# An attention and squared-ReLU kernel: k of tile 0 on ScalarE's queue, distances ahead of identities, six warm-up matmuls

## The chip, the core and the metric

The kernel runs on one core of a Trainium2 chip. The metric is the device time of one execution in microseconds (us). The core's engines run side by side, each with its own list of instructions: TensorE (PE, with its weight loads as PEld), VectorE (DVE), ScalarE (ACT), GpSimd (POOL) and SyncE (SP). They wait for one another, and for transfers, through semaphores. SP, ScalarE and GpSimd can issue transfers (DMAs), which 16 DMA engines then carry out. Line numbers such as L393 are lines of the kernel before; in the changed kernel the same code stands one line earlier from the identities on, or further where it says so.

## What is computed

Windowed causal attention with a linear distance bias, then two matrix products with a squared ReLU between them. Batch 4, 8 heads, 768 positions, 64 elements a head; w_in is 512 x 2048, w_out 2048 x 512. A query sees the 96 latest keys, and the first 8 keys of its sequence:

```python
rel = pos[:, None] - pos[None, :]
is_global = pos[None, :] < n_global          # 8
is_local = (rel >= 0) & (rel < n_local)      # 96
dist = np.where(is_global & ~is_local, n_local, np.abs(rel))
scores = q @ k.T / sqrt(64) - slopes[h] * dist
scores = np.where(is_global | is_local, scores, -1e9)
a = softmax(scores)
x = (a @ v)  # heads side by side: 3072 x 512
out = np.maximum(x @ w_in, 0.0) ** 2 @ w_out # 3072 x 512
```

## The kernel before

The 3072 rows are 24 tiles of 128. For each tile the kernel loads q, k and v, transposes q and k on TensorE (later ones by DMA) into a buffer qkT, makes scores with the tile's own keys and with those of the tile before, exponentiates them on ScalarE, multiplies with v, and normalizes into x on VectorE. Two tiles make a block of 256 rows; for each of the 12 blocks x goes through w_in and w_out, nearly always as seven products of halves in place of eight, which costs VectorE sums and differences and saves TensorE work. Nothing is scheduled at run time: a long table, ORDER, lists every operation of this main part and so fixes the order on every engine. The change leaves that table as it is.

Ahead of the main part stand the preparations, and these the change touches. In the order of the code:

- Tile 0 is loaded as fp32, q and k in one loop (L340), into the buffer plain; both transfers were issued by SP. A small transfer named touch follows (L347). All other q, k and v go through GpSimd's queue, which casts them to bf16; those of the first six tiles are issued at L327.
- VectorE clears a buffer (L382) and sets columns of ones (L385), GpSimd makes a table of position differences, pbi (L388). ScalarE runs a dummy exponential (L390), ahead of which its table is loaded.
- TensorE multiplies the cleared buffer with itself NWARM times, 128 x 512 (L393). The results are not used.
- VectorE makes from pbi two biased copies, pbt (L396) and pbw (L399), the fp32 and the bf16 identity (ident32, printed as ident_96, L402, and ident, L403), and pb, the masked distance, as the smaller of pbt and pbw (L404). pb0 is its own-keys half for a first tile (L406, L408), and a memset gives the global keys their distance in pb (L407). Eight scaled identities sid (L411) add the bias by a matmul (L600) in the first three tiles.
- ScalarE makes E, the exponentials of the distances times the slopes (L418, eight instructions), which later tiles multiply in on VectorE.

The main part begins on TensorE with the transposes of tile 0 (L531, operations tr.0.0 for q and tr.1.0 for k, fp32 with ident32), the bias of tile 0 (L600), transposes of q of tiles 2 and 1, and the scores of tile 0 (L621). ScalarE copies the transposed k (L450), VectorE the transposed q (L452). The transposes of k of tile 1 follow, then the bias of tile 1, the transposes of k of tile 2 and the scores of tile 1. The buffers pbi, pbt, pbw and sid lie inside the buffers named early, and so are printed under that name.

Of the kernel before, what the change touches and what calls it, by code (L numbers as in the profile page):

```python
# [16 lines left out]
Alu = mybir.AluOpType  # L17
# [148 lines left out]
def kernel(  # L166
# [11 lines left out]
    nc = tc.nc  # L178
# [9 lines left out]
    n_global = int(n_global)  # L188
    n_local = int(n_local)
# [26 lines left out]
    def const(shape, dt, name):  # L216
        return consts.tile(shape, dt, name=name, tag=name)
# [26 lines left out]
    pb = const([P, 2, P], BF16, "pb")  # L244
# [5 lines left out]
    pbt = early[:, 0, 2 * P :].rearrange("p (a c) -> p a c", a=2)  # L250
    pbw = early[:, 1, : 2 * P].rearrange("p (a c) -> p a c", a=2)
# [26 lines left out]
    NBUF, NPART = 16, 4  # L278
    SQA = {3, 6}
    NSUM = 2  # L280
    NWARM = 8
    NLATE = 2
    CUT = 3 * d_model // 4
    TWO = (0, 2)
# [35 lines left out]
    def src_rows(x, j):  # L320
        b, t = divmod(j, TPB)
        return x[b, :, t * P : (t + 1) * P, :]
# [14 lines left out]
    for j in range(NPLAIN):  # L337
        for n, src in ((0, q), (1, k)):
            t_ = plain_all[:, n]
            nc.sync.dma_start(  # L340
                out=t_.rearrange("p (h d) -> p h d", h=H),
                in_=src_rows(src, j).rearrange("h p d -> p h d"),
            )
            plain[n, j] = t_
            land["qk"[n], j] = 4.5 + 1.1 * n
# [45 lines left out]

    for i in range(NWARM):
        nc.tensor.matmul(out=banks[7], lhsT=zero[:, :P], rhs=zero, start=True, stop=True)  # L393
# [3 lines left out]
        out=pbt, in0=pbi, scalar=MASK_VAL, in1=pbi, op0=Alu.mult, op1=Alu.min  # L397
    )
    nc.vector.tensor_scalar(  # L399
        pbw, pbi, float(n_local - 1), -MASK_VAL, op0=Alu.add, op1=Alu.mult  # L400
    )
    nc.vector.tensor_scalar(ident32, pbi[:, 0, :], 0.0, None, op0=Alu.is_equal)  # L402
    nc.vector.tensor_scalar(ident, pbi[:, 0, :], 0.0, None, op0=Alu.is_equal)  # L403
    nc.vector.tensor_tensor(out=pb, in0=pbt, in1=pbw, op=Alu.min)  # L404

    nc.vector.tensor_copy(pb0, pb[:, 0, :])  # L406
    nc.vector.memset(pb[:n_global, 1, :], float(-n_local))  # L407
    nc.vector.tensor_scalar_max(pb0[:n_global, :], pb0[:n_global, :], float(-n_local))  # L408
    for h in range(H):

        nc.vector.scalar_tensor_tensor(  # L411
            out=sid[h], in0=ident32, scalar=float(slopes[h] / scale), in1=ident32,
# [68 lines left out]
    for j in range(NT):  # L481
# [152 lines left out]
        for gs in SETS.get(j, [tuple(range(groups))]):  # L634
            n = 8 * len(gs)
# [746 lines left out]
    for blk in range(NBLK):  # L1382
# [12 lines left out]
        for s, sub, half in order2:  # L1395
# [28 lines left out]
            n = NSTEP * blk + s  # L1424
# [74 lines left out]
```

## Time and profile before

| | us |
|---|---|
| median of 3 runs (lowest, highest) | 197.62 (197.32, 198.61) |
| the profiled execution, its own time | 197.03 |
| its span, first to last instruction | 195.3 |
| TensorE busy in the span | 188.3 |
| VectorE busy | 177.0 |
| ScalarE busy | 158.6 |
| GpSimd busy | 75.1 |

The profile shows one execution. The span is shorter than the device time by what lies around it, 1.73 us. A row of the list in order of time gives the start, the length, the engine, the line, the operation, its output and input and how many such instructions it gathers; in square brackets stands how long the engine was idle ahead of it, and what ended that. The ends of matmuls are modelled, so weight loads (PEld) show TensorE's pace better than matmuls do. A row of SPq is the issue of a transfer, not the transfer.

### The profile page before, as it was taken

The page shows a single profiled execution, that of the slowest core. Times are in us where ns is not written, and L with a number is a line of the kernel's source. Part 1 is how long each engine was busy: PE and PEld are TensorE (multiplying, and loading weights), DVE is VectorE, ACT ScalarE, POOL GpSimd, SP SyncE. Part 2 cuts the span into 40 slices and gives each one's busy share as a digit, 9 for nine tenths or more (in the row PEclk, how much of TensorE's full clock was granted, in tenths as well). Part 3 has the DMA queues.
Part 4 walks back from the last instruction along what each step waited for, and adds up shares of the span by engine and source line. Part 5 has one row for each costly group of instructions (what it writes and reads, how often), then busy time and mean ns, then how long its engine had stood idle before and what let it go on. Part 6 is the DMA issues. An engine that isn't in the chain of part 4 may idle for free.

```text
span 195.3 us, 6863 instructions
## 1 busy us (share of the span) xinstructions
PE 188.3 (96%) x2808; PEld 171.1 (88%) x2808; DVE 177.0 (91%) x395; ACT 158.6 (81%) x331; POOL 75.1 (38%) x93
## 2 busy tenths in 40 slices
PE   7986999999999999999999999999999999999993
PEld 3865999999889989989989999998888999999882
DVE  8478999999999999999999999978999999998960
ACT  6798899999989897999997968675987979666511
POOL 8999965747575039056230009290000000000000
PEclk9999999999999999999999999999999999999999
DMA  8999999999999999999999349999855402100055
GB/s 130 149 155 174 177 201 202 204 159 158 179 159 126 147 161 191 136 240 135 142 240 84 77 91 104 198 171 206 166 104 118 134 5 57 54 3 0 0 192 187
DMA packets 111713, 26.92 MB, mean 138 GB/s; under 512 B 103234, under 2 KB 108866, under 8 KB 111682
## 3 DMA queue, kind: packets, MB, share of 16 engines
q0 software_dynamic: 80256, 13.37, 91.9%
q1 hardware_dynamic: 31426, 13.11, 32.2%
q8 instruction: 22, 0.36, 0.7%
q14 instruction: 9, 0.07, 0.1%
HBM read 27.26 MB, written 6.29 MB: 172 GB/s over the span
## 4 chain that ended last, share of the span: by engine, by line
PE 82%; DVE 10%; ACT 3%; DMA 2%; issue 1%; ACTq 0%
PE bank L1019 32%; PE bank L1279 32%; PE bank L1140 5%; PE bank L621 5%; PE bank L774 4%; DVE x L809 2%; DVE hsum L1234 2%; DMA xT<-x 2%; PE bank L393 2%; DVE buf L712 2%; PE bank L531 2%; ACT early L687 1%; ACT buf L687 1%; DVE xs L988 1%; DVE early L712 1%
## 5 line engine op out<-in xcount | busy, mean ns | idle before, releaser
L1279 PEld LDWEIGHTS <-hsum 128*128 128x128 bf16 x384 | 35.9, 98 | 3.9
L450 ACT COPY buf<-bank 128x512 f32<-128x512 f32 (+1 forms) x56 | 30.8, 564 | 10.0 <-PE bank L1019 5.8
L1279 PE MATMUL bank<-wsum,hsum 128*128 128x256 bf16 x288 | 37.7, 273 | 0.0
L687 ACT ACTIVATE buf<-bank 128x512 bf16<-128x512 f32 x54 | 30.1, 604 | 2.3 <-PE bank L621 2.3
L1019 PEld LDWEIGHTS <-qk_first 128*128 128x128 bf16 x504 | 30.7, 98 | 1.4 <-DVE xs L988 0.3
L1086 ACT ACTIVATE hs<-buf 128x512 bf16<-128x512 f32 x46 | 28.7, 636 | 3.5 <-DVE buf L1064 3.2
L1019 PEld LDWEIGHTS <-win 128*128 128x128 bf16 x504 | 30.8, 98 | 0.8
L1064 DVE CUSTOM_DVE_ANT_0 buf<-bank,buf 128x512 f32<-128x512 f32 x42 | 28.3, 684 | 1.8 <-ACT early L687 0.7
L1279 PEld LDWEIGHTS <-hs 128*128 128x128 bf16 x288 | 26.7, 98 | 2.7
L331 POOL DMA_DIRECT2D qk<-in_q_dram x18 | 16.0, 889 | 30.1 <-DMA qkT<-qk 25.7
L1279 PE MATMUL bank<-wout,hs 128*128 128x256 bf16 x192 | 26.0, 273 | 0.0
L1019 PE MATMUL bank<-xT,win 128*128 128x128 bf16 x336 | 24.3, 219 | 0.0
L1019 PE MATMUL bank<-xs,qk_first 128*128 128x128 bf16 x336 | 24.1, 219 | 0.2 <-DVE xs L988 0.2
L331 POOL DMA_DIRECT2D v<-in_v_dram x18 | 16.1, 898 | 20.5 <-DVE hsum L1234 14.3
L687 ACT ACTIVATE early<-bank 128x512 bf16<-128x512 f32 x34 | 19.2, 612 | 2.8 <-PE bank L621 2.7
L809 DVE TENSOR_TENSOR x<-bank,rs 128x512 bf16<-128x512 f32 x24 | 16.6, 692 | 0.9
L331 POOL DMA_DIRECT2D qk<-in_k_dram x18 | 16.2, 898 | 2.3 <-DMA wout<-in_moe_w_out_dram 2.3
L1234 DVE TENSOR_TENSOR hsum<-hs 128x1024 bf16<-128x1024 bf16 (+1 forms) x26 | 16.7, 643 | 0.0
L450 ACT COPY part<-bank 128x256 f32<-128x256 f32 x31 | 11.6, 376 | 5.8 <-PE bank L1279 5.6
L1354 DVE TENSOR_TENSOR buf<-bank,part 128x256 f32<-128x256 f32 x29 | 12.1, 419 | 3.6 <-PE bank L1279 3.3
L621 PEld LDWEIGHTS <-qkT 64*128 64x128 bf16 x352 | 10.0, 94 | 3.9 <-issue 2.6
L1279 PE MATMUL bank<-wout,hsum 128*128 128x256 bf16 x96 | 13.3, 273 | 0.0
(93 smaller groups left out, 379.8 us busy)
## 6 DMA issues: line engine op xcount, KB each, us to landing
out_dram<-buf SPq DMA_DIRECT2D x17, 256.0 KB, 2.5
v<-in_v_dram POOLq DMA_DIRECT2D x24, 128.0 KB, 5.6
qk<-in_q_dram POOLq DMA_DIRECT2D x18, 128.0 KB, 4.8
qk<-in_k_dram POOLq DMA_DIRECT2D x18, 128.0 KB, 5.4
wout<-in_moe_w_out_dram POOLq DMA_DIRECT2D x8, 256.0 KB, 10.2
win<-in_moe_w_in_dram POOLq DMA_DIRECT2D x6, 256.0 KB, 6.7
out_dram<-early SPq DMA_DIRECT2D x5, 256.0 KB, 2.8
qk_first<-in_q_dram POOLq DMA_DIRECT2D x5, 128.0 KB, 4.4
```

The costliest lines, as they stand in the source:

```text
L331: nc.gpsimd.dma_start(out=dst, in_=src)
L450: nc.scalar.copy(dst, src)
L621: nc.tensor.matmul(out=tiles["sc", j, odd, g][:, at, :], lhsT=left[j - 1][half, pair, :] if kt else qkT[j % NKT][half, 1, pair, :], rhs=qk ...
L687: nc.scalar.activation(out=tiles[tag, j, g][:, odd], in_=tiles.pop(("sc", j, odd, g)).rearrange("p a c -> p (a c)"), func=Act.Exp, scale=s ...
L809: nc.vector.tensor_tensor(out=x.rearrange("p (b a) c -> p b a c", b=2), in0=po[:, :, :, :D], in1=rs.to_broadcast([P, 2, 4, D]), op=Alu.mult,)
L1019: nc.tensor.matmul(out=tiles["h", blk, g, bank][:, n], lhsT=left_[:, s, k], rhs=right_[:, k], start=opens and n == 0 and k == 0, stop=k == ...
L1064: nc.vector._custom_dve(TENSOR_ADD_SAT, out=hr, in0=src, in1=tiles.pop(("u", blk, g, i)), s0=float("inf"), s1=0.0,)
L1086: nc.scalar.activation(hs, hr, Act.Square)
L1140: nc.tensor.matmul(out=hT[:, c, cols], lhsT=w_in_sb[s][:, kt, c * P : (c + 1) * P], rhs=tiles["xT", blk][:, kt, cols], start=(kt == 0), st ...
L1234: nc.vector.tensor_tensor(out=t[:, i, h], in0=t[:, a, h] if isinstance(a, int) else half_a(blk, *a)[:, h], in1=t[:, b, h] if isinstance(b, ...
L1279: nc.tensor.matmul(out=tiles["acc", blk, bank][:, cols], lhsT=left_[:, s], rhs=right_[:, cols], start=first and s == 0, stop=s == NSTEP - ...
L1354: nc.vector.tensor_tensor(out=o_sb[:, cols], in0=tiles["acc", blk, bank][:, part], in1=tiles["part", blk, other][:, part], op=Alu.add,)
```

## The change

Three edits. The loop at L340 issues q of tile 0 on SP, as before, and k on ScalarE. NWARM goes from 8 to 6. On VectorE pb and its memset go ahead of the two identities.

```diff
-    NWARM = 8
+    NWARM = 6
...
     for j in range(NPLAIN):
         for n, src in ((0, q), (1, k)):
             t_ = plain_all[:, n]
-            nc.sync.dma_start(
+            (nc.sync, nc.scalar)[n].dma_start(
                 out=t_.rearrange("p (h d) -> p h d", h=H),
                 in_=src_rows(src, j).rearrange("h p d -> p h d"),
             )
...
+    nc.vector.tensor_tensor(out=pb, in0=pbt, in1=pbw, op=Alu.min)
+    nc.vector.memset(pb[:n_global, 1, :], float(-n_local))
     nc.vector.tensor_scalar(ident32, pbi[:, 0, :], 0.0, None, op0=Alu.is_equal)
     nc.vector.tensor_scalar(ident, pbi[:, 0, :], 0.0, None, op0=Alu.is_equal)
-    nc.vector.tensor_tensor(out=pb, in0=pbt, in1=pbw, op=Alu.min)
-
     nc.vector.tensor_copy(pb0, pb[:, 0, :])
-    nc.vector.memset(pb[:n_global, 1, :], float(-n_local))
     nc.vector.tensor_scalar_max(pb0[:n_global, :], pb0[:n_global, :], float(-n_local))
```

The start of ScalarE's instructions in the kernel before, from the table load to the exponentials of tile 0's scores (early) and the next copy (qkT_80 holds tile 0, qkT_81 tile 1):

```order
L390 ACT_TABLE_LOAD
L390 ACTIVATE junk<-early 128x1
L418 ACTIVATE E<-pb 128x256 x8
L450 CAST qkT_80<-bank 128x512
L687 ACTIVATE early<-bank 128x512
L450 COPY qkT_81<-bank 128x512
```

and the same place in the changed kernel:

```order
L340 DMA plain<-in_k_dram 128x8x64
L390 ACT_TABLE_LOAD
L390 ACTIVATE junk<-early 128x1
L417 ACTIVATE E<-pb 128x256 x8
L449 CAST qkT_80<-bank 128x512
L686 ACTIVATE early<-bank 128x512
L449 COPY qkT_81<-bank 128x512
```

The issue of k now stands ahead of the table load, and nothing else on ScalarE has moved. On SP the issue of touch follows that of q directly.

VectorE's instructions before, from the first use of pbi to the copy of tile 0's transposed q:

```order
L396 SCALAR_TENSOR_TENSOR early<-early 128x256
L399 TENSOR_SCALAR early<-early 128x256
L402 TENSOR_SCALAR ident_96<-early 128x128
L403 TENSOR_SCALAR ident<-early 128x128
L404 TENSOR_TENSOR pb<-early 128x256
L406 COPY pb_101<-pb 128x128
L407 MEMSET pb 8x128
L408 TENSOR_SCALAR pb_101<-pb_101 8x128
L411 SCALAR_TENSOR_TENSOR early<-ident_96 128x128 x8
L452 CAST qkT_80<-bank 128x512
```

and in the changed kernel:

```order
L396 SCALAR_TENSOR_TENSOR early<-early 128x256
L399 TENSOR_SCALAR early<-early 128x256
L402 TENSOR_TENSOR pb<-early 128x256
L403 MEMSET pb 8x128
L404 TENSOR_SCALAR ident_96<-early 128x128
L405 TENSOR_SCALAR ident<-early 128x128
L406 COPY pb_101<-pb 128x128
L407 TENSOR_SCALAR pb_101<-pb_101 8x128
L410 SCALAR_TENSOR_TENSOR early<-ident_96 128x128 x8
L451 CAST qkT_80<-bank 128x512
```

pb and its memset stand two places ahead, the identities two places later; the instructions are the same and so is their number.

## Prediction

> **What bounds the kernel now.** I read the page first, then the table of stretches, then the instructions in order of time over the first 14 us, which is where all three edits lie.
>
> ```profile
> span 195.3 us, 6863 instructions
> ...
> PE 188.3 (96%) x2808; PEld 171.1 (88%) x2808; DVE 177.0 (91%) x395; ACT 158.6 (81%) x331; POOL 75.1 (38%) x93
> ...
> PE bank L1019 32%; PE bank L1279 32%; PE bank L1140 5%; PE bank L621 5%; PE bank L774 4%; DVE x L809 2%; DVE hsum L1234 2%; DMA xT<-x 2%; PE bank L393 2%; DVE buf L712 2%; PE bank L531 2%; ACT early L687 1%; ACT buf L687 1%; DVE xs L988 1%; DVE early L712 1%
> ```
>
> TensorE ends the span: 82% of the chain that ended last is its work, and the lines that the change touches, the warm-up (L393) and the transposes with those of tile 0 among them (L531), hold 2% each. The stretches say where TensorE is not yet the bound (columns: stretch, its length, then busy us and count for PE, PEld, DVE, ACT, POOL, the granted clock, the busy share of the DMA engines, GB/s):
>
> ```profile
> 4.00:8.00 4.00, 3.97 (x41) 3.31 (x40) 2.29 (x9) 2.91 (x9) 4.00 (x6) 1.00 2.32 152
> 8.00:12.00 4.00, 3.63 (x63) 2.79 (x61) 2.04 (x6) 3.72 (x9) 4.00 (x6) 1.00 2.36 150
> 12.00:16.00 4.00, 3.39 (x68) 2.74 (x69) 3.71 (x10) 3.54 (x8) 4.00 (x6) 1.00 2.39 154
> 16.00:20.00 4.00, 2.69 (x64) 2.36 (x64) 3.48 (x11) 3.11 (x7) 4.00 (x7) 1.00 1.71 181
> 20.00:30.00 10.00, 10.00 (x162) 9.57 (x159) 9.83 (x26) 9.47 (x19) 7.85 (x11) 1.00 1.64 190
> ```
>
> From 20 us on TensorE has no gap, so a shift of everything at 20 us reaches the end nearly whole. In front of that the engines take turns, POOL (which issues the loads of q, k and v) is busy all the time, and the order of the work is written out. What counts is how much earlier or later the chain stands at about 12 us. The order of time:
>
> ```profile
> 0.74 1.28 ACT L390 ACT_TABLE_LOAD   x1 [0.74 <-PEq L1480]
> 0.74 0.45 SPq L340 DMA_DIRECT2D plain<-in_q_dram  x1
> ...
> 1.19 3.60 PE L393 MATMUL bank<-early 128*128 128x512 bf16 x8 [1.19 <-DVE early L382]
> ...
> 1.25 0.57 SPq L340 DMA_DIRECT2D plain<-in_k_dram  x1
> 1.35 1.90 POOL L327 DMA_DIRECT2D qk_first<-in_q_dram  x2 [0.17 <-issue]
> ...
> 3.21 1.78 POOL L327 DMA_DIRECT2D qk_first<-in_k_dram  x2
> ...
> 4.16 0.23 PEld L531 LDWEIGHTS bank<-ident,plain 128*128 128x128 f32 x1 [0.28 <-DVE early L411]
> ...
> 4.58 1.41 PEld L531 LDWEIGHTS bank<-ident,plain 128*128 128x128 f32 x7 [0.20 <-issue]
> ...
> 5.96 0.54 PEld L600 LDWEIGHTS <-early 128*128 128x128 bf16 x8
> ...
> 6.26 0.58 ACT L450 CAST qkT<-bank 128x512 bf16<-128x512 f32 x1 [0.39 <-PE bank L531]
> ...
> 7.05 0.23 PEld L621 LDWEIGHTS <-qkT 64*128 64x128 bf16 x8
> ...
> 7.47 0.23 PEld L531 LDWEIGHTS <-qk_first 128*128 128x128 bf16 x4 [0.20 <-DMA qk_first<-in_k_dram]
> ...
> 8.48 0.32 PEld L531 LDWEIGHTS <-qk_first 128*128 128x128 bf16 x4
> ...
> 12.05 0.22 PEld L531 LDWEIGHTS <-qk_first 128*128 128x128 bf16 x4 [0.59 <-DMA qk_first<-in_k_dram]
> ```
>
> The reader is to see two kinds of limit. Up to 7.05 TensorE's own queue is the limit: warm-ups, the eight fp32 transposes of tile 0, the bias, more transposes, the first scores. At 7.47 it waits for a landing, k of tile 1, and at 12.05 again, for k of tile 3. These are loads of POOL's queue, which no edit touches.
>
> ```profile
> plain<-in_q_dram SPq DMA_DIRECT2D x1, 256.0 KB, 3.2
> plain<-in_k_dram SPq DMA_DIRECT2D x1, 256.0 KB, 3.8
> ...
> qk_first<-in_k_dram POOLq DMA_DIRECT2D x1, 128.0 KB, 4.2
> ```
>
> These are issue rows of the DMA view, the last column being us from issue to landing. q of tile 0 lands at 0.74 + 3.2 = 3.94, k of tile 0 at 1.25 + 3.8 = 5.05, k of tile 1 at 3.21 + 4.2 = 7.41, just ahead of the row at 7.47.
>
> **Six warm-ups.** Eight take TensorE from 1.19 to 4.58, when the next instruction's matmul starts: 0.424 us each. Two fewer free it at 1.19 + 6 x 0.424 = 3.73 instead of 4.58, by 0.85. But q of tile 0 lands at 3.94, so the first weight load of L531 can move from 4.16 to about 3.95 only, and its matmul, no longer behind a warm-up, from 4.58 to about 4.18. The other seven loads and what follows them keep their pace ((5.96 - 4.58) / 7 = 0.20 each, 0.21 while at half rate), so the bias (L600) starts at 3.95 + 8 x 0.21 = 5.63 instead of 5.96. That is **0.3 us** of the 0.85; the rest becomes a wait for q.
>
> **k through ScalarE.** SP issued it 0.51 after q; now ScalarE issues it at about 0.74, beside q. The second half of the transposes wants it at 3.95 + 4 x 0.21 = 4.8. With the old landing at 5.05 that would be a new wait of 0.25; half a microsecond sooner removes it. What it does to the transfers shows in the queues (packets, MB, busy share) in 2.0 to 2.4 us, 2.8 to 3.2, 4.0 to 4.4 (two rows) and 4.4 to 4.8:
>
> ```profile
> q1 hardware_dynamic: 225, 0.06, 62.1%
> ...
> q1 hardware_dynamic: 437, 0.11, 121.0%
> ...
> q0 software_dynamic: 303, 0.04, 151.1%
> q1 hardware_dynamic: 110, 0.02, 41.4%
> ...
> q0 software_dynamic: 469, 0.06, 234.4%
> ```
>
> With q alone under way 225 packets move in 0.4 us, with both 437: the two do not slow each other. Side by side from the start they should end about half a microsecond sooner, near 3.9. Then POOL's loads have the engines to themselves in 4.0 to 4.4 and move some 469 packets instead of 303; 166 packets at 469 per 0.4 us are **0.14 us** for the loads behind. This shift of k of tile 1 is bounded below by 0 (POOL is busy without a break, and its issue times stay) and above by 0.51 (all of POOL's loads move by what k moved). I take 0.14, which is nearest to the rows.
>
> ScalarE pays: an issue took SP 0.45 to 0.57, so the table load would start at about 1.2 to 1.3 instead of 0.74 and end at 2.5 to 2.6. No row here shows an issue on ScalarE. It is covered as long as ScalarE is through before the row at 6.26:
>
> ```profile
> 1.75 0.63 DVE L402 TENSOR_SCALAR ident<-early 128x128 f32<-128x128 int32 x1
> ...
> 2.37 0.41 DVE L404 TENSOR_TENSOR pb<-early 128x256 bf16<-128x256 f32 x1
> ...
> 3.31 2.56 ACT L418 ACTIVATE E<-pb 128x256 bf16<-128x256 bf16 x8 [1.08 <-DVE pb L407]
> 3.40 1.69 DVE L411 SCALAR_TENSOR_TENSOR early<-ident 128x128 bf16<-128x128 f32 x8
> ```
>
> **Distances first.** The same six instructions in another order. pb (0.41) starts at about 1.9 instead of 2.37, its memset follows, and the eight exponentials start when ScalarE has its table, at about 2.8 instead of 3.31, ending near 5.3. ScalarE then waits for the transposes of k as it does now (0.39 ahead of 6.26), so this earns nothing by itself; it pays for the later table load. The fp32 identity, ready at 1.75 + 0.63 = 2.4, becomes ready at about 3.0, still 0.9 ahead of the transposes at 3.95. The scaled identities (L411) have the same number of instructions ahead of them and still end near 5.1, now 0.5 ahead of the bias at 5.63 instead of 0.9. The reorder costs nothing while this cover holds, and at most its 0.6 us if the identity were waited for.
>
> **The sum.** TensorE could reach the transposes of k of tile 1 0.3 us sooner; their data come 0.14 sooner. The smaller counts: at 8.48 and 12.05, where k of tiles 2 and 3 are due just then, all loads have moved by the same. So 0.14 us at 12 us, carried to the end. The profiled execution has 197.03 us with a span of 195.3; 197.03 - 0.14 = 196.9. The median of the runs shown, 197.62, lies 0.59 above the profiled execution, so in its terms **197.5**.
>
> [...] The granted clock reads 1.00 in every row, but durations tell more:
>
> ```profile
> L531 PEld LDWEIGHTS bank<-ident,plain x8: 142/230/230, 4.2 to 5.8; 128*128 128x128 f32 x8
> ```
>
> A 512-column warm-up takes 0.424 us, and the last of tile 0's weight loads, at 5.8, takes 142 ns where the others take 230: TensorE runs at about half rate until then, 4.6 us after its first matmul. [...] Eight warm-ups make 3.4 us, six only 2.5. [...] The trace agrees with a change after some 3.4 to 4.6 us of work, and can't say what counts.
>
> **The rivals.** *The clock rises later*, and it is slower. Place: the bias, transposes and scores from 5.63 to the row at 8.48. At full rate they took 8.48 - 5.96 - 0.20 idle - about 0.1 = 2.2 us; at half rate all through 4.4, so the row at 8.48 would come at 10.0, 1.5 us late; if the rise comes halfway, 0.8. It decides from the point where the delay exceeds the 0.3 won. 0.9 in the middle: 198.5. Against it: the gap is short, and the transposes fill the same time as now. Over 1% (2 us) it would need half rate beyond about 10 us. *Nothing arrives*: POOL's pace alone sets the landings, or ScalarE issues k so late that it lands as before; the 0.3 turns into a longer wait at 7.47. For it: POOL busy 4.00 of 4.00, an issue every 0.9 us. 197.6. *All loads move by 0.5*: the first loads of POOL, issued at 1.35, hardly moved before 4.0, perhaps because the hardware queue held the engines; then TensorE's 0.3 is the smaller. 197.3.
>
> **How the numbers follow.** Forecast 0.50, nothing 0.22, all loads 0.08, the clock 0.20. All but the far end of the clock's case lie within 1% of 197.62, about what a measurement of this kernel tells from no change: faster 0.02 for what I haven't seen, slower 0.05 for a clock that stays low past 10 us, the same 0.93. The range goes from the largest gain less half the spread of the runs (197.32 to 198.61), 197.3 - 0.6 = 196.7, to the middle of the clock's case, 198.6.
>
> **What would show it.** Right: the first weight load of L530 (now L531) near 3.95 with a wait for q ahead of it, the bias near 5.65, k of tile 0 landing before 4.8, the loads of k of tiles 1 to 3 some 0.1 to 0.2 sooner, a wait of 0.2 to 0.4 for k of tile 1, the same groups behind. Wrong: fp32 weight loads of 230 ns followed by bf16 matmuls at twice the pace of now (the clock), k of tile 0 landing at 5 or later (ScalarE's issue), the exponentials of L417 ending past 6, or the transposes of k of tile 1 still at 7.4 or later.

## The result, and the profile after

The change made the kernel slower by a little: 198.55 us in the median (197.02 to 199.64, 20 executions) against 197.66 (197.20 to 199.63, 20 executions), a ratio of 1.0038 with a 95% interval of 1.0019 to 1.0056. 18 of the 20 lie above the median of before, two at 197.0 lie below all of before. Ratios here and below leave out executions over 1.5% above their kernel's fastest. The profiled execution took 198.33 us, with a span of 196.5.

The page of the changed kernel, span and busy times:

```profile
span 196.5 us, 6859 instructions
...
PE 188.7 (96%) x2806; PEld 171.7 (87%) x2806; DVE 175.7 (89%) x395; ACT 158.9 (81%) x331; POOL 75.2 (38%) x93
```

The same engines are as busy as before. The first 14 us of the changed kernel in order of time (start, length, engine, line, operation; L530 is L531 of before, L599 L600, L620 L621, L417 L418, L410 L411):

```profile
0.74 0.48 ACTq L340 DMA_DIRECT2D plain<-in_k_dram  x1
0.74 0.46 SPq L340 DMA_DIRECT2D plain<-in_q_dram  x1
...
1.19 2.74 PE L393 MATMUL bank<-early 128*128 128x512 bf16 x6 [1.19 <-DVE early L382]
...
1.25 1.28 ACT L390 ACT_TABLE_LOAD   x1 [1.25 <-PEq L1479]
...
2.47 0.15 DVE L404 TENSOR_SCALAR ident<-early 128x128 f32<-128x128 int32 x1
...
2.66 2.55 ACT L417 ACTIVATE E<-pb 128x256 bf16<-128x256 bf16 x8
...
4.76 1.57 PEld L530 LDWEIGHTS bank<-ident,plain 128*128 128x128 f32 x8 [1.74 <-DVE early L410]
4.80 1.94 PE L530 MATMUL bank<-ident,plain 128*128 128x128 f32 x8 [0.86 <-DVE early L410]
...
6.32 1.00 PEld L599 LDWEIGHTS <-early 128*128 128x128 bf16 x8
...
6.77 0.59 ACT L449 CAST qkT<-bank 128x512 bf16<-128x512 f32 x1 [1.57 <-PE bank L530]
7.28 0.90 PEld L530 LDWEIGHTS <-qk_first 128*128 128x128 bf16 x8
...
8.37 0.34 PEld L620 LDWEIGHTS <-qkT 64*128 64x128 bf16 x8 [0.20 <-issue]
...
8.91 0.34 PEld L530 LDWEIGHTS <-qk_first 128*128 128x128 bf16 x4 [0.20 <-issue]
...
10.11 0.32 PEld L530 LDWEIGHTS <-qk_first 128*128 128x128 bf16 x4
...
10.54 0.45 PEld L620 LDWEIGHTS <-qkT 64*128 64x128 bf16 x16
```

Two things differ. TensorE is through with the warm-ups at 3.93 and then has **nothing to do for 0.86 us**: the transposes of tile 0 start at 4.76, later than with eight warm-ups (4.16). And behind them it works **at half the pace**: the eight weight loads of the bias take 1.00 us where they took 0.54, the eight transposes behind 0.90 against 0.49. The transposes of k of tile 1 stand at 8.91 (7.47 before), the scores of tile 1 at 10.54 (8.90). From 10 us on the weight loads take what they took before (four in 0.32 at 10.11, as at 8.48 before); the delay stays. The first product with w_in starts at 21.50; before, at 19.77 in the first profile, and at 20.54 and 20.89 in two more profiles of it, so the first one was a quick execution.

The wait ahead of 4.76 is put down to VectorE, but that is the last instruction that happened to end there; in the kernel before, the same weight load ran at 4.16 while L411 lasted to 5.1. The transfers tell what it waited for (issue to landing in the last column):

```profile
plain<-in_k_dram ACTq DMA_DIRECT2D x1, 256.0 KB, 4.5
plain<-in_q_dram SPq DMA_DIRECT2D x1, 256.0 KB, 3.9
```

q of tile 0 now lands at 0.74 + 3.9 = 4.64 instead of 3.94, and the weight load follows 0.1 later.

### The profile page after: what moved, and what is told of

The parts are those of the page before. It is cut to its first block, busy times and chain, and to the rows that moved or that the text cites. A ratio compares the mean times of both kernels' runs of the same rounds, so it can differ in the third digit from the quotient of the medians.

```text
span 196.5 us, 6859 instructions
## 1 busy us (share of the span) xinstructions
PE 188.7 (96%) x2806; PEld 171.7 (87%) x2806; DVE 175.7 (89%) x395; ACT 158.9 (81%) x331; POOL 75.2 (38%) x93
## 3 DMA queue, kind: packets, MB, share of 16 engines
q10 hardware_dynamic: 1040, 0.26, 0.6%
## 4 chain that ended last, share of the span: by engine, by line
PE 91%; DVE 4%; ACT 2%; issue 1%; ACTq 0%
PE bank L1278 38%; PE bank L1018 33%; PE bank L620 6%; PE bank L1139 5%; PE bank L773 5%; PE bank L530 2%; PE bank L599 1%; ACT early L686 1%; ACT buf L686 1%; PE bank L869 1%; DVE x L808 1%; DVE early L410 1%; DVE buf L1063 0%; DVE early L711 0%; DVE qkT L451 0%
## 5 line engine op out<-in xcount | busy, mean ns | idle before, releaser
L331 POOL DMA_DIRECT2D qk<-in_q_dram x18 | 15.9, 885 | 29.2 <-DMA qkT<-qk 24.4
L620 PEld LDWEIGHTS <-qkT 64*128 64x128 bf16 x352 | 10.1, 95 | 3.9 <-issue 2.8
```

The costliest lines, as they stand in the source:

```text
L331: nc.gpsimd.dma_start(out=dst, in_=src)
L620: nc.tensor.matmul(out=tiles["sc", j, odd, g][:, at, :], lhsT=left[j - 1][half, pair, :] if kt else qkT[j % NKT][half, 1, pair, :], rhs=qk ...
```

## The experiments

The theories. *Clock*: the gap in TensorE's work keeps its rate low for longer, and that is the loss. *Landing*: q and k of tile 0 land later, and that alone is the loss. Beside them: six warm-ups are too few whatever follows; ScalarE's queue costs; the new order on VectorE costs. Times are medians in us, 12 executions each unless a single one is named; before, on the same chips, had 197.84, 197.82 and 197.85.

**k on ScalarE, eight warm-ups** (against the change)

```diff
-    NWARM = 6
+    NWARM = 8
```

> The change with eight warm-up matmuls instead of six. [...] Landing theory (q of tile 0 lands 0.7 us later because k on ScalarE's queue shares the engines with it, and this alone costs the time): the transposes start at 4.8 as in the change, 198.3 to 198.6.

197.72, ratio 0.9999 (0.9962 to 1.0036). Its weight loads:

```profile
4.66 0.42 PEld L530 LDWEIGHTS bank<-ident,plain 128*128 128x128 f32 x4 [0.78 <-DVE early L410]
5.23 0.42 PEld L530 LDWEIGHTS bank<-ident,plain 128*128 128x128 f32 x4 [0.15 <-DMA plain<-in_k_dram]
5.62 0.54 PEld L599 LDWEIGHTS <-early 128*128 128x128 bf16 x8
```

The transposes start nearly as late as in the change (4.66), and k lands as late, but the eight loads of the bias take 0.54 and the median is that of before. That is what the clock theory needs: with two more warm-ups the weight loads stand idle for 0.78 us ahead of the transposes, not for 1.74. Taken alone, the interval still touches the change's ratio (1.0036 against 1.0038). The run with ten warm-ups below has q and k as late and stays under it (1.0015 at most, where the change's interval begins at 1.0019). By the two together the landing theory and the one on ScalarE's queue fall.

**Six warm-ups alone** (against before)

```diff
-    NWARM = 8
+    NWARM = 6
```

> The kernel before with six warm-ups and nothing else. Clock theory with the gap as its cause: q lands at 3.9, the gap is about 0.2 us, the rate rises as before; 197.3 to 197.6 us. Landing theory: the same 197.3 to 197.6. A third theory, that six warm-ups are too few whatever follows them (transposes don't count as work): the rate rises late, 198.2 to 198.6.

197.69, a little above the 197.3 to 197.6 expected, ratio 0.9989 (0.9966 to 1.0013): no loss, so six are not too few when q lands in time.

```profile
4.13 0.72 PEld L531 LDWEIGHTS bank<-ident,plain 128*128 128x128 f32 x4 [1.11 <-DVE early L411]
5.21 0.72 PEld L531 LDWEIGHTS bank<-ident,plain 128*128 128x128 f32 x4 [0.36 <-DMA plain<-in_k_dram]
5.91 0.70 PEld L600 LDWEIGHTS <-early 128*128 128x128 bf16 x8
...
7.67 0.23 PEld L531 LDWEIGHTS <-qk_first 128*128 128x128 bf16 x4 [0.28 <-DMA qk_first<-in_k_dram]
```

Nothing is gained either: the transposes start at 4.13, then wait for k (0.36), and at 7.67 for k of tile 1.

**Four warm-ups alone** (against before: 8 becomes 4)

> The kernel before with four warm-ups: both transfers on SP as before, so q lands at 3.9 and TensorE has a gap of about 1.0 us from 2.9. Clock theory: the rate rises late in most executions, 198.0 to 198.7 us, and the weight loads of the bias stay at half pace. Landing theory: nothing lands later and the transposes start 0.4 us sooner, 197.2 to 197.6.

199.21, above the clock theory's 198.0 to 198.7; 11 of 12 executions lie above the median of before. The ratio, 1.0028 (0.9995 to 1.0062), is taken over nine of the twelve and is not clear of 1, so the loss in time is likely here and not shown. The profile shows the pace:

```profile
4.22 0.71 PEld L531 LDWEIGHTS bank<-ident,plain 128*128 128x128 f32 x4 [2.04 <-DVE early L411]
5.43 0.72 PEld L531 LDWEIGHTS bank<-ident,plain 128*128 128x128 f32 x4 [0.49 <-DMA plain<-in_k_dram]
6.13 1.01 PEld L600 LDWEIGHTS <-early 128*128 128x128 bf16 x8
...
8.72 0.35 PEld L531 LDWEIGHTS <-qk_first 128*128 128x128 bf16 x4 [0.20 <-issue]
```

Here both transfers are on SP, and still the weight loads stand idle for 2.04 us, the bias has its loads in 1.01 and the transposes of k of tile 1 stand at 8.72. The half pace comes here behind a gap alone; ScalarE isn't needed.

**The new order on VectorE alone** (against before)

```diff
+    nc.vector.tensor_tensor(out=pb, in0=pbt, in1=pbw, op=Alu.min)
+    nc.vector.memset(pb[:n_global, 1, :], float(-n_local))
     nc.vector.tensor_scalar(ident32, pbi[:, 0, :], 0.0, None, op0=Alu.is_equal)
...
-    nc.vector.tensor_tensor(out=pb, in0=pbt, in1=pbw, op=Alu.min)
...
-    nc.vector.memset(pb[:n_global, 1, :], float(-n_local))
```

> The distances ahead of the identities and nothing else (SP issues both, eight warm-ups). Clock and landing theories: no effect, 197.5 to 197.8 us. A theory in which the later identity or the earlier exponentials cost the time: 198.2 or more.

198.01, a little above the 197.5 to 197.8 expected, ratio 1.0007 (0.9985 to 1.0029): no effect on the time that can be measured. There is one in the trace, on GpSimd, for whose loads TensorE waits. Its first two issues now last 1.99 us instead of 1.90, and its later issues in the first 8 us start 0.11 to 0.12 later:

```profile
1.35 1.99 POOL L327 DMA_DIRECT2D qk_first<-in_q_dram  x2 [0.17 <-issue]
3.33 1.76 POOL L327 DMA_DIRECT2D qk_first<-in_k_dram  x2
```

So it is in all seven profiles with the new order (the second pair at 3.32 or 3.33) and in none of the six with the old one (3.21 or 3.22).

**The change with k issued later** (against the change)

```diff
-            (nc.sync, nc.scalar)[n].dma_start(
+            if n == 0:
+                nc.sync.dma_start(
...
     nc.scalar.activation(junk, zero[:, :1], Act.Exp)
+    nc.scalar.dma_start(
+        out=plain_all[:, 1].rearrange("p (h d) -> p h d", h=H),
+        in_=src_rows(k, 0).rearrange("h p d -> p h d"),
+    )
```

> The change with one difference: ScalarE issues k of tile 0 behind its table load and the dummy exponential, at about 2.2 us instead of 0.74, so that q of tile 0 has the transfer engines to itself at first. Six warm-ups, the same queue, the same order on VectorE. [...] A theory in which ScalarE's queue or the count of six costs the time: 198.3 to 198.8 as in the change. [...]

198.05, ratio 1.0007 (0.9974 to 1.0041). ScalarE issued k at 1.17, beside its table load, not at 2.2 as I had thought. That is 0.43 later than in the change, and enough: q lands at 0.74 + 3.3, the first transposes start at 4.17 and the eight loads of the bias take 0.67.

```profile
plain<-in_q_dram SPq DMA_DIRECT2D x1, 256.0 KB, 3.3
...
4.17 0.71 PEld L535 LDWEIGHTS bank<-ident,plain 128*128 128x128 f32 x4 [1.15 <-DVE early L415]
...
5.96 0.67 PEld L604 LDWEIGHTS <-early 128*128 128x128 bf16 x8
```

Of the 12 executions 5 lie at 198.8 to 199.5; whether a part of the loss remains, these few don't tell. The profile is that of a start without the long gap (0.27 us ahead of the first transposes, 0.86 in the change): the same count of six and the same queue as in the change, and the bias at nearly full pace.

**The change once more**

> The change itself once more, for a second profile and on the chip of the other three. All theories: 198.3 to 198.8 us in the median, with a few executions near 197.0. Clock theory: if this profile's execution is a slow one, q lands at 4.5 to 4.8, TensorE has a gap of about 0.9 us, and the bias of tile 0 has its weight loads at half pace (8 in 1.0 us); if it is one of the few near 197.0, the eight take 0.55 us in spite of the gap.

198.66, ratio 1.0033 (1.0004 to 1.0062): the loss holds. By luck the profiled execution, 197.75, is the quickest of the 12:

```profile
4.70 0.94 PEld L530 LDWEIGHTS bank<-ident,plain 128*128 128x128 f32 x8 [1.67 <-DVE early L410]
4.73 1.15 PE L530 MATMUL bank<-ident,plain 128*128 128x128 f32 x8 [0.79 <-DVE early L410]
5.61 0.54 PEld L599 LDWEIGHTS <-early 128*128 128x128 bf16 x8
...
7.54 0.23 PEld L530 LDWEIGHTS <-qk_first 128*128 128x128 bf16 x4 [0.30 <-DMA qk_first<-in_k_dram]
```

This is the same kernel with q as late (4.70) and nearly the same gap (0.79), and in this execution TensorE was at full rate from the first transpose of tile 0 on (0.94 for the eight weight loads, 1.57 in the first profile). What was expected of a quick execution, the eight loads of the bias in 0.55 in spite of the gap, came (0.54). The transposes of k of tile 1 stand at 7.54 instead of 8.91, the first product with w_in at 20.60 instead of 21.50, and the execution took 0.58 us less. So within one and the same kernel the earlier rise of the rate goes with 0.9 us less at the first product with w_in, and there the delay of the change is gone. It is one pair, and executions of before differ by as much (197.03 to 198.07) without a difference in the rate of the bias.

**q on ScalarE, k on SP, eight warm-ups** (against the change)

```diff
-            (nc.sync, nc.scalar)[n].dma_start(
+            (nc.scalar, nc.sync)[n].dma_start(
...
-    NWARM = 6
+    NWARM = 8
```

> q of tile 0 on ScalarE's queue, k on SP's, eight warm-ups, distances first: for the landings, not the time. If the second queue to ask starts late whichever engine it is, or the two share the transfer engines evenly, q lands at 4.5 or later here too and k on SP at about 4.7. If ScalarE's queue is the slower one (its packets began 0.7 us behind SP's in the change), q on it lands at 5.0 or later, and k on SP at about 4.6.

One execution, 198.96. Its landings:

```profile
plain<-in_q_dram ACTq DMA_DIRECT2D x1, 256.0 KB, 4.6
plain<-in_k_dram SPq DMA_DIRECT2D x1, 256.0 KB, 4.0
```

ScalarE's transfer is again the later one, by 0.6, though issued at the same time; so it is the slower queue here and not just the second to ask, and the transfer on SP again takes 4.0, not 3.2. Its time says little: it had another wait, of 1.6 us at 15.9, for a load of POOL's.

**The change with ten warm-ups**

> The change with ten warm-ups: TensorE is busy without a gap from 1.2 to 5.4, past the landing of q (4.7) and of k (5.2). Clock theory: no gap, so the rate rises as in the kernel before, and only the 0.6 to 0.8 us by which the transposes start late are lost where the loads of tile 1 don't hide them: 197.7 to 198.3 us, below the change with its six. Landing theory, or one in which ScalarE's queue costs: at or above the change, 198.5 to 199.

197.83, ratio 0.9982 (0.9949 to 1.0015): as before, and below the change, as the clock theory has it (197.7 to 198.3). One of the twelve executions, 387.0, stands out, is not in the ratio, and is told at the end.

**Before, twice more, and with seven warm-ups**

> The kernel before, for a second profile, since its first one (197.03 us) lies below its median. Clock theory: TensorE has no gap ahead of the transposes, so the rate rises between about 4 and 7 us and the transposes of k of tile 1 stand at 7.4 to 7.9; 197.2 to 198.0 us. Question beside it: from the transposes of k of tile 3 at 12.05 to the first product with w_in the first profile took 7.7 us, the profiles of the variants some 0.7 more. If the first profile was a lucky execution, this one shows the longer stretch too; if the variants share a loss there, it shows 7.7 again.

> The kernel before, a third profile, for the same two questions as the second: 197.2 to 198.0 us, the transposes of k of tile 1 at 7.4 to 7.9 us, and the stretch behind 12.05 us as in the second.

> The kernel before with seven warm-ups, which end at about 4.16, when q has landed: no gap, and TensorE may start on tile 0 up to 0.4 us sooner. Clock theory: the rate rises as before, and k of tile 1 sets the time at 7.4 to 7.7 anyway: 197.4 to 197.8 us, no change that can be measured. If the warm-ups beyond the landing of q do cost time, 197.2 to 197.4.

197.96 and 198.07, single executions. From the transposes of k of tile 3 (12.29 and 12.09) to the first product with w_in they took 8.25 and 8.80 us, the first profile 7.72, so the first profile of before was a lucky one. In the second, the transposes of k of tile 1 came at 8.06, outside the 7.4 to 7.9 expected: k of tile 0 took 4.8 to land there, not 3.8, so landings, too, differ by up to 1 us between executions of one kernel. Seven warm-ups: 197.74, ratio 1.0004 (0.9979 to 1.0030), no change. The third profile of before shows why sparing TensorE time there earns nothing:

```profile
5.67 0.54 PEld L600 LDWEIGHTS <-early 128*128 128x128 bf16 x8
...
7.86 0.23 PEld L531 LDWEIGHTS <-qk_first 128*128 128x128 bf16 x4 [0.78 <-DMA qk_first<-in_k_dram]
```

Its bias started 0.3 sooner than in the first profile, just what the prediction hoped for, and all of it and more went into the wait for k of tile 1. No version that beats both kernels came out.

**The rate over all profiles.** The trace also records when TensorE's clock went to full rate. Twelve of the thirteen profiles have such a record. Beside it stand, from the rows of the weight loads, how long these were idle ahead of the first transposes of tile 0 and what the eight loads of the bias of tile 0 took:

| profile | idle, us | eight loads of the bias, us | full rate from, us |
|---|---|---|---|
| before | 0.28 | 0.54 | 5.82 |
| before_again | 0.27 | 0.54 | 6.02 |
| before_third | 0.30 | 0.54 | 4.11 |
| change | **1.74** | 1.00 | **9.37** |
| change_again | 1.67 | 0.54 | **4.17** |
| k_act_warm8 | 0.78 | 0.54 | 4.32 |
| only_warm6 | 1.11 | 0.70 | 6.24 |
| only_reorder | 0.42 | 0.82 | 6.70 |
| only_warm4 | **2.04** | 1.01 | **9.09** |
| only_warm7 | 0.68 | 0.78 | 6.52 |
| k_act_late | 1.15 | 0.67 | 6.21 |
| swap_warm8 | 1.57 | 0.54 | 5.28 |

In the eight profiles with an idle time of 1.15 us or less full rate came between 4.11 and 6.70. In the four with 1.57 or more it came either at 9.09 and 9.37 or, at 4.17 and 5.28, ahead of the transposes (4.70 and 5.46), within the gap. The amount of work alone does not tell the two apart: in change_again the rate rose when TensorE had done its 2.74 us of warm-ups, in the first profile of the change not behind the same 2.74 and 1.94 of transposes. What sets the moment of the rise was not shown. Where it came ahead of the transposes the gap cost nothing in the pace, and that differs from execution to execution.

## Why the prediction was wrong

The forecast was 0.14 us less and the kernel became 0.9 slower in the medians, 0.75 by the ratio (0.0038 x 197.66). The likeliest case was the wrong one. The range's upper end, 198.6, still held the time, because it reached to the rival that came true.

- **The step that failed: "With q alone under way 225 packets move in 0.4 us, with both 437: the two do not slow each other."** The rise from 225 to 437 was no second transfer joining in. Each of the two is 1040 packets, and before, SP's queue had begun 1046 by 3.13 us, so k's had hardly begun; in 2.4 to 2.8 us q alone moved 403. In the run with k issued later it moved 407 in that stretch; in the change 274, and 240 in the next 0.4 us, beside 45 and 162 of k (q1 is SP's queue, q10 ScalarE's; first before, then the later k, then the change in both stretches):

```profile
q1 hardware_dynamic: 403, 0.10, 112.7%
...
q1 hardware_dynamic: 407, 0.10, 114.1%
...
q1 hardware_dynamic: 274, 0.07, 76.4%
q10 hardware_dynamic: 45, 0.01, 12.7%
...
q1 hardware_dynamic: 240, 0.06, 67.5%
q10 hardware_dynamic: 162, 0.04, 45.4%
```

  One transfer alone moves as much (407) as the two side by side (240 + 162 = 402). In one queue k's packets came behind q's; in two queues they share, and q, which is needed first, lost 0.7 us, while k landed at 0.74 + 4.5 = 5.24, no sooner than its 5.05. From the later q came the gap of 0.86, where the prediction had reckoned with 0.2, and from the gap, in the first profile, the late rise of the rate.
- **Six warm-ups, 0.3 sooner:** failed by the same step in the change: with q at 4.64 the bias came at 6.32 instead of 5.96, later and not sooner. Six alone had q at 0.74 + 3.3 = 4.04 and its first load at 4.13; its bias came at 5.91, hardly sooner than 5.96, since the second half of the transposes waited for k on SP. So no run has shown the 0.3 for six warm-ups.
- **All loads 0.14 sooner:** no. Transfers of tile 0 ended no earlier, and k of tile 1 was not used sooner in any profile of the variants (7.54 at best, 7.47 before). POOL's issue times, which the prediction took to stay, moved 0.11 to 0.12 later with the new order on VectorE (k of tile 1 at 3.33 instead of 3.21).
- **TensorE's time ahead of 7.5 us is worth nothing, POOL's landings are:** right in the main. Ten profiles had the rise before 7 us; in eight of them TensorE then waited for k of tile 1. The two others, only_reorder and swap_warm8, came to it at 7.83 and 7.76 without a wait.
- **ScalarE pays half a microsecond, the exponentials cover it; the order on VectorE costs nothing:** right as far as ScalarE and VectorE go. Table load at 1.25, exponentials from 2.66 to 5.21, identity ready by 2.6. What the order cost lay elsewhere, the 0.11 us on POOL; in the time it does not show, with a ratio of the order alone of 1.0007 (0.9985 to 1.0029).
- **The clock's rival:** right in place and in effect: in the first profile of the change full rate came at 9.37, 3.55 later than in that of before (5.82). Its reason was only half right: not that six warm-ups are too few in themselves (six alone lost nothing), but the gap behind them. Its size, 0.9 us in the middle of its case against 0.75 to 0.89 measured, agrees in part by luck: the row at 8.48 came at 10.11, the 1.6 late of its far end, and the kernel lost about half of that. Its chance of 0.20 came from a gap of 0.2 us, that is, from the landing at 3.94. With a gap of 0.86 it is the likely case. The 3.4 to 4.6 us of work that the prediction took from one trace are no bound: in change_again the rate rose behind 2.74. What counts as work, it left open, and the runs leave it open too: with six warm-ups alone the rate rose at 6.24, when some 2.2 us of transposes were done, in change_again at 4.17, ahead of all of them.

## What to carry to other kernels

Here the warm-up work had to last until real work could follow, so its number hung on the landing of the first operand (3.94 us before, 4.64 in the change): check both together, and let it rather overlap by one than leave a gap, since two warm-ups more cost nothing that could be measured here (eight against six: 0.9989, 0.9966 to 1.0013, for six; ten in the change: 0.9982) and the change, with its 0.86 us of idleness, lost 0.9 us in the median. A second queue was no second set of engines here (402 packets in 0.4 us from two queues, 407 from one): q, which was needed first, landed 0.7 us later beside k in another queue than ahead of it in the same one. When executions of one kernel differ by as much as the effect, take several profiles and compare executions of the same kernel that went the two ways.

## What was not expected

- ScalarE's queue was slower to start than SP's. Issued at the same 0.74, SP's first packets moved at 1.87 and ScalarE's at 2.55 in the change; with q and k swapped, at 1.87 and 2.41.
- In the run with k issued later ScalarE issued the transfer while its own table load ran (1.17, in the load from 0.74 to 2.02), though it stands behind it in the code.
- In one execution with ten warm-ups, which was the profiled one, the trace has no record of full rate: the eight loads of the bias took 0.99, and the execution took 387.0 us, about twice as long. Why is open; it came once, and in no other kernel. Its page, and a group of its matmuls that take 273 ns in the profile of before:

```profile
span 385.2 us, 6867 instructions
...
L1278 PE MATMUL bank<-wsum,hsum 128*128 128x256 bf16 x288 | 74.7, 448 | 0.0
```

- The table of stretches gave a granted clock of 1.00 for that execution too, and for the stretches at half pace ahead of the rise (5.95 to 9.37 in the change): the pace of weight loads and matmuls told the rate (1.00 for the eight loads of the bias against 0.54), the column did not.
